# Attention and a SiLU feed-forward on one core: scores computed key-major, exponentials without a shift under a checked bound, SiLU on ScalarE, and an instruction order written by hand

## The chip, the cores and the metric

The kernel runs on 1 of the cores of a Trainium2 chip. The metric is the device time of one execution in microseconds (us); lower is better. PE is the matrix engine (TensorE) and PEld its weight loads, DVE is VectorE, ACT is ScalarE, POOL is GpSimd, SP is the engine whose queue issues the DMAs.

## The reference

Inputs: q, k, v of shape (8, 12, 448, 64) in float32, gains g_q and g_k of 64 elements, and two weight matrices, w_in (768 x 2048) and w_out (2048 x 768), which arrive as float64.

```python
def rmsnorm(x, g):
    return x / np.sqrt(np.mean(x * x, axis=-1, keepdims=True) + 1e-06) * g
q_n, k_n = rmsnorm(q, g_q), rmsnorm(k, g_k)
scores = (1.0 / np.sqrt(64)) * np.matmul(q_n, k_n.transpose(0, 1, 3, 2))
scores = scores - np.max(scores, axis=-1, keepdims=True)
attn = np.exp(scores)
attn = attn / (np.sum(attn, axis=-1, keepdims=True) + 1e-09)
x = np.matmul(attn, v)                     # then heads side by side: (3584, 768)
h = x @ w_in
out = (h / (1.0 + np.exp(-h))) @ w_out     # (3584, 768), float32
```

The gains come from `np.abs(np.random.randn(64)) + 0.5` with a fixed seed; the largest product of a g_q element with its g_k element is 5.26.

## The kernel before

All products are in float32. Work goes by pairs of heads: two heads of 64 features fill the 128 partitions, so there are 8 batches of 6 pairs, 48 pairs in all, numbered n. S is 448 rows, cut into J = 4 groups of R = 112.

For a pair, `load` brings q, k and v. `normalise` squares the rows on GpSimd, sums on VectorE, raises to the power -0.5 on GpSimd and multiplies on GpSimd. `transpose_qk` puts features on partitions with PE transposes; VectorE evicts them. Then, for each of the four query groups c, `scores` makes a 112 x 448 block for either head with queries on partitions (L204), VectorE takes the row maxima (L208), ScalarE computes exp with that maximum as bias and a row sum (L212), and VectorE divides the rows (L216 to L220). `transpose_attn` turns the block over with eight PE transposes (L230), since the sum over keys needs keys on partitions; VectorE (L233) and ScalarE (L235) evict. After the four groups, `weighted_sum` multiplies by v (L245) and leaves the pair's part of x transposed.

The feed-forward part runs one batch behind. `feed_forward` is a generator: 16 blocks f of the hidden layer, each a chain of 6 products with w_in (L282) and then `silu`, which takes one exp on ScalarE (L263) and four operations on VectorE, among them a reciprocal of a 128 x 448 tile (L265); after that, 3 or 4 tiles of 128 tokens by two halves, each a chain of 16 products with w_out (L294), a copy (L303) and a store. An even batch has 3 such tiles, an odd batch 4, as what is left over of two batches is joined. `fill` draws from the generator so many streamed columns after each piece of attention, so that PE has work while the softmax runs. It has nothing to draw in the first batch. After the last pair the last batch's feed-forward runs alone.

During the first batch the weights are brought in and rounded from float64 to float32 in 40 pieces (`load_weights`, `round_weights`: one ScalarE, four VectorE and one GpSimd operation a piece, L123 to L141). The order of instructions on an engine comes from a scheduler, which starts from the order of the code and moves instructions by its own costs.

In float32 a product is two instructions on PE (L282: 768 products, 1536 instructions); a transpose is one.

Of the kernel before, what the change touches and what calls it, by code (L numbers as in the profile page):

```python
# [17 lines left out]
# High words of float64 read as float32: that of 2**-127, and the last one under 2**128's.  # L18
HIGH_MIN = 2.0**-15
HIGH_MAX = 122880.0 - 2.0**-7  # L20


@with_exitstack
def kernel(
# [18 lines left out]
    B, H, S, D = q.shape  # L43
    DM, DFF = w_in.shape
    P = 128
    J = 4  # rows of a sequence that stand side by side on one partition
    R = S // J
    NPAIR = H // 2
    NW = DM // P
    NF = DFF // P  # L50
    HALF = DM // 2
    FULL = S // P  # whole token tiles of a batch; what is over is joined with the next batch's
    REST = S - FULL * P
    assert 2 * D == P and J * R == S and 2 * REST == P and NW == NPAIR and B % 2 == 0

    const = ctx.enter_context(tc.tile_pool(name="const", bufs=1))
    ld = ctx.enter_context(tc.tile_pool(name="ld", bufs=2))
    at = ctx.enter_context(tc.tile_pool(name="at", bufs=2))
    mp = ctx.enter_context(tc.tile_pool(name="mp", bufs=2))
# [5 lines left out]
    ident = const.tile([P, P], F32, name="ident")  # L65
    make_identity(nc, ident)
    minus_half = const.tile([P, 1], F32, name="minus_half")
    nc.gpsimd.memset(minus_half, -0.5)
    # Both gains and the scale of the scores, as one factor per feature of a pair of heads.
# [3 lines left out]
    for t, g in ((gq2, g_q), (gk2, g_k)):  # L73
        for half in range(2):
            nc.sync.dma_start(t[ds(half * D, D), :], g.rearrange("(d one) -> d one", one=1))
# [5 lines left out]
    W1 = const.tile([P, NW, DFF], F32, name="W1")  # L81
    W2 = const.tile([P, NF, DM], F32, name="W2")
    COLS = 512
    pieces = [
        (W1[:, c, ts(i, COLS)], w_in[ts(c, P), ts(i, COLS)])
        for i in range(DFF // COLS)
        for c in range(NW)
    ] + [(W2[:, f, :], w_out[ts(f, P), :]) for f in range(NF)]
    raws = []
    # The second part's own tile, which nothing needs before the weights are there.  # L90
    stage = mp.tile([P, NF * FULL * P], F32, name="g_own", bufs=1).bitcast(I32)
    NRAW, NLOW = 3, 2
    assert NRAW * 2 * DM + NLOW * DM == NF * FULL * P

    def load_weights():
        """The next piece as it comes: float32 to its place, bits of float64 to the stage."""
        if len(raws) == len(pieces):
            return
        dst, src = pieces[len(raws)]
        raw = None  # L100
        if src.dtype == I64:
            raw = stage[:, ds(len(raws) % NRAW * 2 * DM, 2 * dst.shape[-1])]
# [279 lines left out]
```

## Time and profile before

| | before |
|---|---|
| runs (us) | 1970.28, 1974.19, 2138.64; median 1974.19 |
| profiled execution | span 1967.9 us from first to last instruction; the profile has no other time for it |
| busy | PE 1812.2 us, PEld 920.5, DVE 1347.9, ACT 511.9, POOL 437.9 |
| first product of the feed-forward (L282) | at 235.10 us |
| last batch's feed-forward alone, from | 1809.16 us |

The two close runs lie 2.4 and 6.3 us above the span. The span has three stages: the first batch's attention with the rounding of the weights, up to 235 us; the attention of batches 1 to 7 with the feed-forward of batches 0 to 6 between it, 1574 us; and the last feed-forward, 159 us. Rows of the timeline give the start and the length of a group of instructions; since matmuls overlap at their ends, the step from one group's start to the next is what counts.

### The profile page before, as it was taken

The numbers are of one execution on the slowest core, as the hardware profiler recorded it, in microseconds if no ns is written. First come the engines' busy times: TensorE is split into PE (matmuls) and PEld (weight loads), VectorE is DVE, ScalarE is ACT, GpSimd is POOL, SyncE is SP. The second block draws the span as 40 slices with busy tenths as digits, with TensorE's granted clock in tenths as the row PEclk, the third lists the DMA queues.
The fourth block names the chain that finished last, engine by engine and source line by source line (L and its number), as shares of the span: only waits on it lengthen the run. The fifth ranks groups of instructions, "written<-read, shape, count | busy, mean of one in ns | idle before, by whom it ended". The sixth has DMA issues, their size and how long they took to land.

```text
span 1967.9 us, 18858 instructions
## 1 busy us (share of the span) xinstructions
PE 1812.2 (92%) x6784; PEld 920.5 (47%) x6784; DVE 1347.9 (68%) x2433; ACT 511.9 (26%) x1233; POOL 437.9 (22%) x335
## 2 busy tenths in 40 slices
PE   3654899999999999999999999999999999999999
PEld 2222344554445544454445544454445544454555
DVE  6999699538973499637983389745994379843930
ACT  2333222222222232222222222222222223222100
POOL 5567312211221211211121131121112111210000
PEclk9755799999999999999999999999999999999999
DMA  4454000100000000110001010010001000000000
GB/s 147 147 163 163 28 14 15 37 27 18 24 23 31 27 29 14 32 31 18 15 23 36 26 30 17 19 40 23 14 15 40 27 23 19 14 13 13 0 12 20
DMA packets 48796, 70.42 MB, mean 36 GB/s; under 512 B 4160, under 2 KB 43584, under 8 KB 48704
## 3 DMA queue, kind: packets, MB, share of 16 engines
q1 hardware_dynamic: 48704, 69.22, 11.4%
q8 instruction: 54, 0.88, 0.2%
q14 instruction: 38, 0.31, 0.1%
HBM read 58.20 MB, written 11.01 MB: 35 GB/s over the span
## 4 chain that ended last, share of the span: by engine, by line
PE 52%; DVE 38%; ACT 6%; POOL 2%; issue 1%; DMA 1%; SPq 0%; ACTq 0%; POOLq 0%
PE mm L294 24%; DVE s L265 12%; PE mm L282 11%; PE sc L204 6%; PE tr L230 6%; ACT e L212 5%; DVE nmax L208 5%; DVE e L220 5%; PE mm L245 5%; DVE g_own L271 2%; DVE qT L192 2%; DVE s L264 2%; DVE aT L233 2%; DVE total L216 1%; DVE x L261 1%; DVE rms L168 1%
## 5 line engine op out<-in xcount | busy, mean ns | idle before, releaser
L282 PE MATMUL mm<-xT,W 128*128 128x448 f32 x1536 | 627.6, 553 | 0.0
L294 PE MATMUL mm<-W,g_own 128*128 128x384 f32 x1536 | 530.3, 492 | 0.0
L208 DVE TENSOR_REDUCE nmax<-sc 112x1 f32<-112x448 f32 x384 | 224.2, 615 | 306.8 <-PE sc L204 306.4
L282 PEld LDWEIGHTS mm<-xT,W 128*128 128x128 f32 x1536 | 281.1, 192 | 286.3 <-issue 286.3
L212 ACT ACTIVATE e<-sc,nmax 112x448 f32<-112x448 f32 x384 | 241.0, 631 | 537.1 <-DVE nmax L208 533.2
L265 DVE RECIPROCAL s<-s 128x448 f32<-128x448 f32 x128 | 377.1, 2946 | 2.4
L294 PEld LDWEIGHTS mm<-W,g_own 128*128 128x128 f32 x1536 | 279.3, 190 | 209.4 <-issue 47.2
L230 PE MATMUL tr<-ident,e 112*112 112x112 f32 x1536 | 204.2, 276 | 91.6 <-DVE e L220 53.3
L230 PEld LDWEIGHTS tr<-ident,e 112*112 112x112 f32 x1536 | 160.7, 141 | 224.6 <-issue 131.7
L204 PE MATMUL sc<-kT,qT 64*112 64x448 f32 x768 | 226.9, 623 | 40.3 <-ACT e L212 38.2
L167 POOL TENSOR_TENSOR qn<-q 112x512 f32<-112x512 f32 x48 | 51.2, 1066 | 944.4 <-PE tr L188 938.3
L173 POOL TENSOR_TENSOR rms<-rms,minus_half 112x8 f32<-112x8 f32 x96 | 168.2, 1761 | 282.3 <-DVE rms L169 282.2
L235 ACT COPY aT<-tr 112x448 f32<-112x448 f32 x192 | 101.9, 530 | 374.9 <-PE tr L230 374.9
L233 DVE COPY aT<-tr 112x448 f32<-112x448 f32 x192 | 115.9, 604 | 84.6 <-PE tr L230 84.5
L220 DVE TENSOR_SCALAR e<-e,total 112x448 f32<-112x448 f32 x384 | 167.4, 478 | 4.7
L245 PE MATMUL mm<-aT,v 112*64 112x448 f32 x768 | 160.9, 562 | 0.3 <-DVE aT L233 0.3
L263 ACT ACTIVATE s<-x 128x448 f32<-128x448 f32 x128 | 73.5, 574 | 227.9 <-DVE x L261 227.9
L204 PEld LDWEIGHTS sc<-kT,qT 64*112 64x112 f32 x768 | 61.8, 181 | 142.9 <-issue 65.8
L216 DVE TENSOR_SCALAR total<-total 112x2 f32<-112x2 f32 x192 | 49.0, 255 | 100.4 <-ACT e L212 100.4
L245 PEld LDWEIGHTS mm<-aT,v 112*64 112x64 f32 x768 | 53.2, 141 | 103.9 <-issue 71.3
L294 PE MATMUL mm<-W,g_joint 128*128 128x384 f32 x256 | 87.8, 490 | 0.0
L261 DVE TENSOR_SCALAR x<-mm 128x448 f32<-128x448 f32 x128 | 78.2, 611 | 8.7 <-PE mm L282 8.3
(35 smaller groups left out, 983.3 us busy)
## 6 DMA issues: line engine op xcount, KB each, us to landing
g_own<-in_moe_w_in_dram SPq DMA_DIRECT2D x24, 512.0 KB, 4.0
g_own<-in_moe_w_out_dram SPq DMA_DIRECT2D x16, 768.0 KB, 4.5
q<-in_q_dram SPq DMA_DIRECT2D x48, 224.0 KB, 2.6
k<-in_k_dram SPq DMA_DIRECT2D x48, 224.0 KB, 2.7
v<-in_v_dram SPq DMA_DIRECT2D x48, 224.0 KB, 2.6
out_dram<-o SPq DMA_DIRECT2D x56, 192.0 KB, 1.9
gq<-in_g_q_dram SPq DMA_DIRECT2D x2, 0.2 KB, 2.3
gk<-in_g_k_dram SPq DMA_DIRECT2D x2, 0.2 KB, 2.3
```

What stands on the lines that cost most here:

```text
L173: nc.gpsimd.tensor_tensor(out=flat, in0=flat, in1=minus_half[0:R].to_broadcast([R, 2 * J]), op=ALU.pow)
L204: nc.tensor.matmul(ps[h], st["qT"][r, ts(c, R)], st["kT"][r, :], start=True, stop=True)
L208: nc.vector.tensor_reduce(out=nmax[:, h : h + 1], in_=ps[h], axis=AX.X, op=ALU.max, negate=True)
L212: nc.scalar.activation(e, ps[h], AF.Exp, bias=nmax[:, h : h + 1], accum_out=total[:, h : h + 1])
L220: nc.vector.tensor_scalar_mul(out=e, in0=e, scalar1=total[:, h : h + 1])
L230: nc.tensor.transpose(ps[:, j, :], st["e"][h][:, ts(j, R)], ident[0:R, 0:R])
L233: nc.vector.tensor_copy(dst, ps)
L235: nc.scalar.copy(dst, ps)
L245: nc.tensor.matmul(ps[ds(h * D, D), :], st["v"][:, h, j, :], st["aT"][h][:, j, :], start=(j == 0), stop=(j == J - 1),)
L265: nc.vector.reciprocal(out=s, in_=s)
L282: nc.tensor.matmul(h, W1[:, c, ts(f, P)], xT[b][:, c, :], start=(c == 0), stop=(c == NW - 1))
L294: nc.tensor.matmul(ps, g[:, f, :], W2[:, f, ts(half, HALF)], start=(f == 0), stop=(f == NF - 1),)
```

## The change

- **A branch at run time.** The largest product of the gains is computed on chip and compared with 7.5. If it is not above, the scores cannot exceed 60 and `bounded` runs; else `general`, which keeps the row maxima and the old softmax and is not interleaved by hand.
- **Key-major scores.** In `bounded` a score block has keys on partitions: `scores` makes 112 keys x 448 queries for both heads into two PSUM banks, and one ScalarE exp of 112 x 896 evicts it. No maxima, no sum, no division there and no transposes of the attention: `weigh` multiplies the block by v directly.
- **Sums and division.** `add_up` adds the four blocks of a head, head 0 on VectorE and head 1 on GpSimd. `divide` multiplies the sums by a tile of ones on PE, so that the sum stands in all 64 partitions of a head, takes the reciprocal on VectorE (128 x 448, once a pair) and multiplies the unloaded product with it.
- **SiLU on ScalarE** in one function, straight from PSUM, as two activations (384 and 64 columns). The output copies go to VectorE.
- **Rounding** moves one VectorE operation to ScalarE (the absolute value), works in 56 pieces, and is spread over the first ten pairs: 2 pieces a pair in batch 0, 12 a pair after that. Raw w_in lies in the space of w_out until that is needed.
- **PSUM**: scores 2 x 2 banks, `tr` 1, `av` 1, `mm` 2 (before: 2, 2, and 4 for `mm`).
- **Order**: no scheduler moves instructions; each engine runs them as the code issues them. Queries are permuted inside a batch, and the stores undo that, in two DMAs a tile.

The core of the diff, new code only (what it replaces is printed above):

```diff
+    taken = nc.values_load(small[:1, :1], min_val=0, max_val=1)
+    with tc.If(taken > 0) as cond:
+        with tc.manual_schedule():
+            bounded(**arm())
+    with cond.Else():
+        general(**arm())
...
+    def transpose(n, name):
+        t = ps.tile([P, S], F32, name="tr")
...
+        if name == "q":
+            nc.vector.tensor_copy(dst, t)
+        else:
+            nc.vector.tensor_scalar_mul(out=dst, in0=t, scalar1=gains)
+    def scores(n, half):
+        st = state[n]
+        for j in range(2 * half, 2 * half + 2):
+            banks = ps.tile([R, 2, BANK], F32, name="sc", bufs=2)
+            for h in range(2):
+                r = ds(h * D, D)
+                nc.tensor.matmul(banks[:, h, 0:S], st["kT"][r, ts(j, R)], st["qT"][r, :],
+                                 start=True, stop=True)
+            st["e", j] = at.tile([R, 2, S], F32, name="e", bufs=5)
+            nc.scalar.activation(st["e", j], banks[:, :, 0:S], AF.Exp)
+    def weigh(n, half):
+        if half == 0:
+            st["av"] = ps.tile([P, S], F32, name="av")
+        for j in range(2 * half, 2 * half + 2):
+            for h in range(2):
+                nc.tensor.matmul(st["av"][ds(h * D, D), :], st["v"][:, h, j, :],
+                                 st["e", j][:, h, :], start=(j == 0), stop=(j == J - 1))
+    def add_up(n, half):
+        for h, eng in ((0, nc.vector), (1, nc.gpsimd)):
+            es = st["es"][h]
+            if half == 0:
+                eng.tensor_tensor(out=es, in0=st["e", 0][:, h, :], in1=st["e", 1][:, h, :], op=ALU.add)
+            else:
+                for j in (2, 3):
+                    eng.tensor_tensor(out=es, in0=es, in1=st["e", j][:, h, :], op=ALU.add)
+    def unload(n):
+        nc.scalar.copy(st["xU"], st["av"])
+    def divide(n):
+        t = ps.tile([P, S], F32, name="tr")
+        for h in range(2):
+            nc.tensor.matmul(t[ds(h * D, D), :], ones[0:R, :], st["es"][h], start=True, stop=True)
+        r = at.tile([P, S], F32, name="r")
+        nc.vector.reciprocal(out=r, in_=t)
+        nc.vector.tensor_tensor(out=xT[b][hp], in0=st["xU"], in1=r, op=ALU.mult)
...
+            for dst, cols in (
+                (own[:, f, :], ds(odd * z.REST, z.FULL * P)),
+                (joint[:, f, ds(odd * z.REST, z.REST)], ds((1 - odd) * z.FULL * P, z.REST)),
+            ):
+                nc.scalar.activation(dst, h[:, cols], AF.Silu)
...
+    for n, (b, hp) in enumerate(pairs):
+        rounds = [1, 0, 1, 0] if b == 0 else [3, 3, 3, 3]
+        load(n + 2)
+        scores(n, 0)
+        for _ in range(rounds[0]):
+            weights.round(weights.NRAW)
+        fill()
+        if n > 0:
+            divide(n - 1)
+            if hp == 0:
+                begin(b - 1, 4 * z.NPAIR - 1)
+        weigh(n, 0)
+        scores(n, 1)
+        add_up(n, 0)
+        for _ in range(rounds[1]):
+            weights.round(weights.NRAW)
+        fill()
+        transpose(n + 1, "q")
+        weigh(n, 1)
+        unload(n)
+        add_up(n, 1)
+        for _ in range(rounds[2]):
+            weights.round(weights.NRAW)
+        fill()
+        transpose(n + 1, "k")
+        normalise(n + 2)
+        for _ in range(rounds[3]):
+            weights.round(weights.NRAW)
+        fill()
+    divide(last)
```

How the order changes is seen best on three engines.

PE, in a stretch where the feed-forward multiplies by w_out. Before, one query group and a half of a pair (`sc` are the scores, `tr` transposes, `mm` the feed-forward; a row counts products):

```order
L204 MATMUL sc<-kT,qT 112x448 x2
L294 MATMUL mm<-W_92,g_own 128x384 x4
L188 MATMUL tr<-ident,qn 128x112 x4
L188 MATMUL tr<-ident,kn 128x112 x4
L294 MATMUL mm<-W_92,g_own 128x384
L230 MATMUL tr<-ident,e_5081 112x112 x4
L230 MATMUL tr<-ident,e_5084 112x112 x4
L294 MATMUL mm<-W_92,g_own 128x384 x4
L204 MATMUL sc<-kT,qT 112x448 x2
```

After, a whole pair (`av` is the product with v, `tr<-es,ones` the sum product):

```order
L316 MATMUL sc<-qT,kT 112x448 x4
L402 MATMUL mm<-W_82,g_own 128x384 x9
L365 MATMUL tr<-es,ones 64x448 x2
L330 MATMUL av<-e,v_63 64x448 x4
L316 MATMUL sc<-qT,kT 112x448 x4
L402 MATMUL mm<-W_82,g_own 128x384 x9
L302 MATMUL tr<-ident,qn 128x112 x4
L330 MATMUL av<-e,v_63 64x448 x4
L402 MATMUL mm<-W_82,g_own 128x384 x9
L302 MATMUL tr<-ident,kn 128x112 x4
L402 MATMUL mm<-W_82,g_own 128x384 x9
```

The feed-forward comes in four runs a pair instead of eight, the transposes of e are gone, and a run of nine products stands between the scores and the product that needs their exponentials.

ACT, in a stretch where the feed-forward multiplies by w_in. Before (`s` is the exp of the SiLU, `e` that of the scores, `aT` an evicted transpose):

```order
L212 ACTIVATE e_5379,total<-sc,nmax 112x448
L212 ACTIVATE e_5382,total<-sc,nmax 112x448
L263 ACTIVATE s<-x 128x448
L235 COPY aT_5352<-tr 112x4x112
L263 ACTIVATE s<-x 128x448
L212 ACTIVATE e_5448,total<-sc,nmax 112x448
L212 ACTIVATE e_5451,total<-sc,nmax 112x448
```

After (`g_own` and `g_joint` are the SiLU's outputs, `xU` the unloaded product):

```order
L321 ACT_TABLE_LOAD
L321 ACTIVATE e<-sc 112x896 x2
L394 ACT_TABLE_LOAD
L394 ACTIVATE g_own<-mm 128x384
L394 ACTIVATE g_joint<-mm 128x64
L321 ACT_TABLE_LOAD
L321 ACTIVATE e<-sc 112x896 x2
L394 ACT_TABLE_LOAD
L394 ACTIVATE g_own<-mm 128x384
L394 ACTIVATE g_joint<-mm 128x64
L394 ACTIVATE g_own<-mm 128x384
L394 ACTIVATE g_joint<-mm 128x64
L356 COPY xU<-av 128x448
```

Exp and SiLU need different function tables, so a table load stands at each change between them; before, there was one in the whole program. The branch that runs has 88.

DVE, in the first batch. Before (`W` are weights being rounded):

```order
L216 TENSOR_SCALAR total<-total 112x2
L130 TENSOR_SCALAR W_91<-W_91 128x512
L217 RECIPROCAL total<-total 112x2
L130 TENSOR_SCALAR W_91<-W_91 128x512
L220 TENSOR_SCALAR e_244<-e_244,total 112x448
L220 TENSOR_SCALAR e_247<-e_247,total 112x448
L138 SCALAR_TENSOR_TENSOR W_91<-g_own,W_91 128x512 x2
L233 COPY aT_167<-tr 112x4x112
L208 TENSOR_REDUCE nmax<-sc 112x1 x2
```

After, one pair:

```order
L121 TENSOR_SCALAR W_81<-W_81 128x512
L124 TENSOR_SCALAR W_81<-W_81 128x512
L128 SCALAR_TENSOR_TENSOR W_81<-W_82,W_81 128x512
L369 RECIPROCAL r<-tr 128x448
L371 TENSOR_TENSOR xT<-xU,r 128x448
L346 TENSOR_TENSOR es<-e 112x448
L306 COPY qT<-tr 128x448
L351 TENSOR_TENSOR es<-es,e 112x448 x2
```

A piece of rounding now stands ahead of the reciprocal and another ahead of the eviction of the next pair's keys (L308); in the first batch they are 12 pieces instead of 40.

More of the change, by code (lines that the diff above doesn't have):

```diff
@@ new lines @@
+    weights = Weights(nc, const, w_in, w_out, z)
+    for _ in range(weights.NRAW):
+        weights.load()
+    ident = const.tile([P, P], F32, name="ident")
+    make_identity(nc, ident)
+    ones = const.tile([P, D], F32, name="ones")
+    nc.gpsimd.memset(ones, 1.0)
+    minus_half = const.tile([P, 1], F32, name="minus_half")
+    nc.gpsimd.memset(minus_half, -0.5)
+    small = const.tile([1, 1], I32, name="small")
+    most = const.tile([1, 1], F32, name="most")
+    both = const.tile([1, D], F32, name="both")
@@ L76 @@
-    nc.vector.scalar_tensor_tensor(
-        out=gains, in0=gq2, scalar=float(D) ** -0.5, in1=gk2, op0=ALU.mult, op1=ALU.mult
-    )
[L81 to L91, printed above, removed]
```

515 lines of the change are left out of this document (340 added, 175 removed).

## The prediction, made before the changed kernel ran

> **What bounds the kernel now.** I read the page's busy shares first, then the slices over time, then a table of stretches.
>
> ```profile
> PE 1812.2 (92%) x6784; PEld 920.5 (47%) x6784; DVE 1347.9 (68%) x2433; ACT 511.9 (26%) x1233; POOL 437.9 (22%) x335
> PE   3654899999999999999999999999999999999999
> DVE  6999699538973499637983389745994379843930
> PEclk9755799999999999999999999999999999999999
> 17.00:235.00 218.00, 132.21 (x445) 62.04 (x446) 192.32 (x374) 76.97 (x170) 127.36 (x81) 0.68 0.41 130
> 235.00:1812.00 1577.00, 1525.81 (x5893) 773.67 (x5892) 1080.07 (x1971) 419.24 (x1036) 300.59 (x240) 0.99 0.08 24
> ```
>
> There are two limits. In the first five slices, the first batch, PE is half idle at a clock of 0.5 to 0.7 and VectorE is full (192 of 218 us: rounding and softmax). From 235 us on PE is busy for 1526 of 1577 us at clock 0.99: whatever leaves PE there leaves the time. A busy PE is not yet a priced one, so I price its steps from the starts of groups on PE's own timeline, in the middle of the program and around its ends.
>
> ```profile
> 1051.04 1.01 PE L204 MATMUL sc<-kT,qT 64*112 64x448 f32 x4
> 1051.98 3.49 PE L294 MATMUL mm<-W,g_own 128*128 128x384 f32 x10
> 1055.31 0.55 PE L188 MATMUL tr<-ident,qn 112*128 112x112 f32 x4
> 1055.69 0.55 PE L188 MATMUL tr<-ident,kn 112*128 112x112 f32 x4
> 1056.08 0.82 PE L294 MATMUL mm<-W,g_own 128*128 128x384 f32 x2
> 1056.92 1.09 PE L230 MATMUL tr<-ident,e 112*112 112x112 f32 x8
> 1057.85 2.76 PE L294 MATMUL mm<-W,g_own 128*128 128x384 f32 x8
> ...
> 1064.89 3.23 PE L245 MATMUL mm<-aT,v 112*64 112x448 f32 x16
> 1068.05 0.98 PE L230 MATMUL tr<-ident,e 112*112 112x112 f32 x8
> 1068.87 4.05 PE L294 MATMUL mm<-W,g_own 128*128 128x384 f32 x12
> ...
> 235.10 3.19 PE L282 MATMUL mm<-xT,W 128*128 128x448 f32 x8
> 1809.16 61.15 PE L282 MATMUL mm<-xT,W 128*128 128x448 f32 x162
> 1949.80 14.35 PE L294 MATMUL mm<-W,g_own 128*128 128x384 f32 x44
> ```
>
> From these: a w_in instruction takes 61.15/162 = 0.377 us, a w_out instruction 14.35/44 = 0.326. Four score instructions, both heads at once, take 1051.98 - 1051.04 = 0.94 us; the 16 with v 3.16; a set of q or k transposes 0.38 or 0.39; eight transposes of e 0.93 or 0.82, say 0.87. Ten w_out instructions cost 3.33 us from start to start, 0.07 more than 10 x 0.326: a restart of the feed-forward costs about 0.1.
>
> A pair of before then costs 4 x 0.94 + 3.16 + 0.77 + 4 x 0.87 + 8 x 0.1 = 11.97 us of PE. The seven feed-forwards between 235.10 and 1809.16: w_in 7 x 192 x 0.377 = 507; w_out 4 x 192 x 0.326 + 3 x 256 x 0.326 = 501. With 42 pairs, 503, the sum is 1511 of 1574 us. So **63 us there are waits**. The waits of PE in that stretch name most:
>
> ```profile
> PE tr L230 <- DVE qT L192: 28.0, 19, 2.1
> PE tr L230 <- DVE e L220: 21.6, 58, 0.9
> ```
>
> Both are waits of the transposes of e, for the divided block and for the eviction queued with it on VectorE.
>
> **Stage 2, step by step.** The transposes of e go: 4 x 0.87 = 3.48 us a pair. The scores keep their streams (eight blocks a pair, two at a time) but come in two runs of 8 instructions: 0.94 and another 0.75 (two streams of 0.377), so 1.69 a run, 3.38 a pair for 3.76. The product with v is split in two, 3.16 + 0.1. Transposes of q and k are split, 0.77 + 0.1. The sum product is new: two chains side by side, like four score instructions, 0.94. Restarts fall to four, 0.4. The pair: 3.38 + 3.26 + 0.87 + 0.94 + 0.4 = 8.85 us. Saved: 42 x (11.97 - 8.85) = **131 us**.
>
> Now the waits. Feed-forward runs last (507 + 501)/(7 x 23 fills) = 6.3 us. Between the scores and the product that reads their exponentials stands such a run, so I cost the exponentials at nothing if ScalarE gets them out within it. The rows for that:
>
> ```profile
> L212 ACT ACTIVATE e<-sc,nmax 112x448 f32<-112x448 f32 x384 | 241.0, 631 | 537.1 <-DVE nmax L208 533.2
> L123 ACT ACTIVATE g_own<-g_own 128x512 int32<-128x512 uint32 x24 | 16.1, 671 | 66.4 <-POOL W L141 52.2 <-DMA g_own<-in_moe_w_in_dram 14.2
> L123 ACT ACTIVATE g_own<-g_own 128x768 int32<-128x768 uint32 x16 | 14.6, 913 | 28.3 <-POOL W L141 25.7 <-DMA g_own<-in_moe_w_out_dram 2.6
> L303 ACT COPY o<-mm 128x384 f32<-128x384 f32 x56 | 26.8, 479 | 114.3 <-PE mm L294 112.8
> L123 ACT ACT_TABLE_LOAD x1 | 1.3, 1283 | 0.7 <-PEq L366 0.7
> ```
>
> No row has an exp of 896 elements: twice 631 is the upper end, 631 itself the lower; the two L123 rows differ by 0.242 us for 256 elements, so 631 + 448 x 0.945 = 1.05 us, which I take. A SiLU block: 0.48 (the 384-element copy) plus some 0.2 for 64 elements. In a pair that multiplies by w_in, ScalarE then has 4 x 1.05 + 0.53 (unload) + 5.3 blocks x 0.68 + 4 table loads x 1.28 = 13.5 us of about 33. After the scores its longest sequence is a table load and two exponentials, 3.4 us, inside the 6.3; if a SiLU stands ahead too, 4.1. `mm` has two banks instead of four: a chain of six products lasts 4.5 us, and the SiLU of the chain before it ends within 1 us, or 5 us where exponentials stand ahead of it, in which case 3.3 us of attention lie on PE as well. That should hold.
>
> VectorE and `tr`, which has one bank for the q transposes, the k transposes and the sums:
>
> ```profile
> L265 DVE RECIPROCAL s<-s 128x448 f32<-128x448 f32 x128 | 377.1, 2946 | 2.4
> L271 DVE TENSOR_TENSOR g_own<-x,s 128x384 f32<-128x384 f32 x128 | 69.8, 545 | 0.1
> L196 DVE TENSOR_SCALAR kT<-tr,gains 128x448 f32<-128x448 f32 x48 | 30.7, 639 | 0.0
> L138 DVE SCALAR_TENSOR_TENSOR W<-g_own,W 128x512 int32<-128x512 int32 x24 | 17.9, 750 | 0.0
> L130 DVE TENSOR_SCALAR W<-W 128x512 int32<-128x512 int32 x24 | 11.6, 488 | 0.0
> L127 DVE TENSOR_SCALAR W<-W 128x512 f32<-128x512 f32 x24 | 10.4, 441 | 0.0
> L141 POOL TENSOR_TENSOR W<-W,g_own 128x512 int32<-128x512 int32 x24 | 33.0, 1378 | 40.9 <-DVE W L138 27.5 <-DVE total L216 8.8 <-ACT aT L235 3.8
> L173 POOL TENSOR_TENSOR rms<-rms,minus_half 112x8 f32<-112x8 f32 x96 | 168.2, 1761 | 282.3 <-DVE rms L169 282.2
> ```
>
> The reciprocal holds `tr` for 2.95 us; the next user, the q transposes, comes 1.6 + 1.7 + 6.3 us later, so it is hidden; the 128 reciprocals of the SiLU become 48. A pair costs VectorE 2.95 + 0.55 + 6 small operations of about 0.6, below 10 us of 33.
>
> The tight pairs are those from 6 to 9, where the other 44 pieces are rounded. A piece takes 2 x 0.67 us on ScalarE, 0.44 + 0.49 + 0.75 = 1.68 on VectorE, 1.38 on GpSimd; for pair 6, 12 pieces: 16 us, 20 us and 17 us on top of 13, 9 and 9. Each stays under PE's 33, but pieces now stand ahead of reciprocals. I followed pair 6: the reciprocal starts behind three pieces, at 9.5 us, and the first feed-forward chain waits 2.8 us for its last operand. w_out pieces, of 384 elements, are lighter. I take **20 us of waits** in all of stage 2 (4 in pair 6, 16 elsewhere) with bounds of 0 and 110: nothing waits, or the 63 of before remain and pairs 6 to 9 take another 12 each.
>
> Stage 2: 507 + 501 + 42 x 8.85 + 20 = **1400 us** for 1574.
>
> **Stage 1.** Before, six pairs ran in (235 - 17)/6 = 36.3 us each, held by VectorE. Now VectorE has two pieces and one pair, 3.4 + 10 = 13 us, and the chain decides. Its clock: PE was at half speed here, so scores take 3.0 us a run and v 3.1. The chain from the first scores: j0's exp ends at 2.9, j1's at 4.4; the ScalarE part of a piece at 5.7, VectorE's at 7.4; the reciprocal behind it at 10.35, and the q transposes wait for its bank; then v for the second half up to 14.3, unload 14.9, the second piece on ScalarE 16.3 and VectorE 18.0, and only then the eviction of the next keys, 18.7. With handovers between engines I take 19 us a pair, 114 for six. At full clock the same chain gives 17.4 without handovers; a floor is VectorE's 13, and a third more on everything is 25: **84 to 150 us** with the start.
>
> The start itself:
>
> ```profile
> 6.68 1.04 POOL L167 TENSOR_TENSOR qn<-q 112x512 f32<-112x512 f32 x1 [5.38 <-DMA q<-in_q_dram]
> 17.29 1.84 PE L204 MATMUL sc<-kT,qT 64*112 64x448 f32 x4 [1.11 <-DVE kT L196]
> ```
>
> Normalising began at 6.68 us on the arrival of q and scores at 17.29. Now it also waits for the gains, three small VectorE operations, a register load and a branch on every engine. The trace has no such branch; between nothing and another such 10 us I take 3. So pair 0 starts at 20, pair 6 at 134; before, the feed-forward started at 235. Saved: 101 us.
>
> **Stage 3.** 192 x 0.377 + 256 x 0.326 = 156 us, the same instructions; 1809.16 + 156 leaves 2.9 us for the last copy and store. The last reciprocal (2.95 + 0.55) lies beside five of the first chain's products. 159 us, half a microsecond more than nothing lost.
>
> **The sum.** 20 + 114 + 1400 + 159 = 1693 us of span, 275 less than 1967.9: 131 from PE work, 43 from waits, 101 from the first stage. The median of the runs is 6.3 above the span; this gives **1699 us**.
>
> **A rule that speaks against it.** 88 table loads stand where one stood; by the row they are 88 x 1.28 = 113 us, all on an engine that was busy for 26%. The Trainium skill, page "ScalarE: Activation LUTs", section "What ACT_TABLE_LOAD costs", puts every switch at about 2.66 us, as a drain of 1.38 comes on top of 1.28, and advises grouping calls by table set. The load itself agrees with this row (1283 ns); no run here shows the drain. By that price, an estimate from the page, a w_in pair would need 19 us of ScalarE instead of 13.5 and only pairs 6 and 7 would come out over PE's time, by about 15 us in all: 1714.
>
> **The rivals.**
> - *Table switches reach PE.* If every switch delays an exponential or frees a bank late, 88 x 1.28 = 113 us come back: 1812 us. For it: they stand right ahead of the exponentials in ScalarE's order. Against: 13.5 of 33 us.
> - *The first batch stays long*, its in-order chain waiting on rounding as before: 6 x (36.3 - 19) = 104 us more, 1803. For it: two pieces stand in each pair's chain. Against: 12 pieces instead of 40.
> - *Slower: the runs of feed-forward don't cover the exponentials.* It decides once ScalarE is more than 6.3 us late with them; then PE runs the stage 1 chain and the fills one after the other, 18.7 + 24 = 42.7 us a pair for 33: 42 x 9.9 = 416 us more, 2115. Against: waits of this kind (L204 and L230 on ACT or DVE) were 50 us before with less distance.
> - *The branch takes `general`.* It would need a gain product above 7.5, and the largest is 5.26. Without interleaving, 48 pairs of some 20 us, eight feed-forwards of about 146 and 56 pieces of some 1.4 us come to 2200.
>
> **How the numbers follow.** The forecast has 0.85, table switches 0.07, the long first batch 0.05, slower 0.02, `general` 0.01. The range takes in the bounds of the unknown costs: down to no waits and the short first stage, 1699 - 20 - 30 = 1649; up to 90 more of waits, 1789, or 36 more of the first stage with half of those, so I end it at 1790. Left out are the 0.15 of the rivals and a little of the forecast with both bounds at once. Within 2% (about what a measurement of this kernel can tell from no change: 1935 to 2014) only the first two rivals together reach, 1699 + 113 + 104 = 1916 and a slow rounding stage: 0.02. Slower has the last two, 0.03; faster 0.95.
>
> **What would show it.** Right: w_in products begin near 137 us; from there on PE is at 98% or more with a clock of 0.99, L316 and L330 show hardly any wait for ACT, and the last feed-forward begins near 1534 and takes 159. Wrong: waits of PE for L321 (table switches, or fills too short) or for L306 and L308 (rounding ahead of evictions); a first stage of pairs above 25 us; a pair's PE work above 8.85 in the timeline, which would make the 131 us too large.

## The result, and the profile after

| | before | after |
|---|---|---|
| median (us) | 1972.24 (1968.46 to 2138.64, 4 runs) | 1707.88 (1707.17 to 1709.11, 4 runs) |
| ratio after/before | | 0.8671, 95% interval 0.8658 to 0.8683 |
| span of the profiled execution | 1967.9 | 1707.3 |
| time of that execution | 1970.28 | 1709.11 |

The run of 2138.64 us was a slow one, and the ratio leaves it out. The forecast was 1699 us, with a range of 1649 to 1790. It holds, 9 us low. `bounded` was the branch taken: only its lines appear in the trace.

First the page of after: busy shares, and two rows of the slices.

```profile
PE 1609.5 (94%) x5440; PEld 792.0 (46%) x5440; DVE 577.3 (34%) x708; ACT 438.9 (26%) x696; POOL 583.5 (34%) x448
PE   4668688999999999999999999999999999999998
PEclk9878888999999999999999999999999999999999
```

VectorE's 1348 us have become 577, and PE has 203 us less to do. Of the opening, seven slices of 43 us are below nine tenths now, none but the first below six; before, four slices of 49 us were at three to six tenths, most of them at a granted clock of 0.5 to 0.7, which is now 0.7 to 0.9. Cut at pair 0's scores, pair 6's scores, the last wait of PE and the last feed-forward, the table of stretches reads (columns: stretch, its length, busy time and instructions of PE, PEld, VectorE, ScalarE and GpSimd, granted clock of PE, DMA share, GB/s):

```profile
18.93:124.90 105.97, 68.73 (x261) 24.29 (x261) 79.21 (x94) 39.22 (x55) 81.24 (x59) 0.81 0.36 107
124.90:281.30 156.40, 118.33 (x352) 51.73 (x353) 109.49 (x153) 78.99 (x141) 85.60 (x70) 0.85 0.35 99
281.30:1546.65 1265.35, 1265.35 (x4373) 629.67 (x4371) 376.43 (x441) 310.96 (x469) 407.77 (x306) 1.00 0.10 29
1546.65:1707.30 160.65, 155.11 (x450) 84.96 (x448) 8.50 (x11) 9.68 (x32) 0.00 (x0) 0.99 0.04 12
```

From 281 us to the last feed-forward PE is busy without a gap at full clock: nothing there can be won but by less PE work. Whatever was lost against the forecast was lost before 281 us, in pairs 0 to 9. PE's waits by cause (total us, times, longest) and the starts on its timeline that mark the stages:

```profile
PE mm L386 <- ACT g_joint L394: 31.7, 5, 11.0
PE sc L316 <- DVE kT L308: 24.4, 7, 5.6
PE tr L302 <- POOL qn L287: 15.4, 1, 15.4
PE tr L302 <- DVE r L369: 10.4, 5, 2.6
PE mm L386 <- DVE xT L371: 6.4, 1, 6.4
PE tr L302 <- DVE qT L306: 3.2, 4, 1.1
PE av L330 <- ACT e L321: 0.9, 1, 0.9
```

```profile
106.97 3.33 PE L316 MATMUL sc<-qT,kT 64*112 64x448 f32 x8 [3.87 <-DVE kT L308]
124.90 3.30 PE L316 MATMUL sc<-qT,kT 64*112 64x448 f32 x8 [3.35 <-DVE kT L308]
132.33 4.03 PE L386 MATMUL mm<-xT,W 128*128 128x448 f32 x10
```

The 15.4 us are the start. L308, L302 and L306 belong almost wholly to the first batch, whose pairs are 17.9 us apart (124.90 - 106.97) instead of 36.3. The first two rows that matter beyond it are the new ones: **38 us in which the feed-forward waits**, 31.7 of them for a SiLU (L394): `mm` has two banks, and PE can't begin the next chain of products before the SiLU has read one. Between 124 and 290 us no other wait of PE is above 3.3.

Why a SiLU of 0.7 us is 11 us late is told by ScalarE's timeline at the longest of the five waits, with PE's row under it and then rows of GpSimd and of VectorE (in brackets the idle time ahead of a row, and what ended it):

```profile
177.33 0.56 ACT L119 ACTIVATE last<-raw 128x384 int32<-128x384 uint32 x1 [9.94 <-POOL W L132]
177.79 0.54 ACT L120 ACTIVATE W<-raw 128x384 f32<-128x384 f32 x1
178.34 1.28 ACT L394 ACT_TABLE_LOAD   x1
179.63 0.49 ACT L394 ACTIVATE g_own<-mm 128x384 f32<-128x384 f32 x1
180.02 0.22 ACT L394 ACTIVATE g_joint<-mm 128x64 f32<-128x64 f32 x1
```

```profile
180.29 3.35 PE L386 MATMUL mm<-xT,W 128*128 128x448 f32 x4 [11.01 <-ACT g_joint L394]
```

```profile
168.68 1.11 POOL L287 TENSOR_TENSOR qn<-q,rms 112x512 f32<-112x512 f32 x1
169.75 1.03 POOL L287 TENSOR_TENSOR kn<-k,rms 112x512 f32<-112x512 f32 x1
170.75 2.66 POOL L132 TENSOR_TENSOR W<-W,W 128x512 int32<-128x512 int32 x2
...
176.31 0.99 POOL L132 TENSOR_TENSOR W<-W,last 128x384 int32<-128x384 int32 x1 [0.94 <-issue]
```

```profile
167.40 0.43 DVE L124 TENSOR_SCALAR W<-W 128x512 int32<-128x512 int32 x1
...
168.93 3.37 DVE L124 TENSOR_SCALAR W<-W 128x512 int32<-128x512 int32 x1
```

A w_out piece begins on ScalarE by writing `last`, a scratch tile in two slots, and ends on GpSimd, where L132 reads it. The third w_out piece of a group therefore waits on ScalarE until GpSimd has finished the first (176.31 + 0.99 = 177.30; ScalarE goes on at 177.33). ScalarE runs in order, so the SiLU that PE waits for stands behind that piece, though its own input was ready long before: PE had done its last product ahead of the wait by 169.28 (180.29 - 11.01).

### The profile page after: what moved, and what is told of

It reads as the page before. It is cut to its first block, busy times and chain, and to the rows that moved or that the text cites. A ratio compares the mean times of both kernels' runs of the same rounds, so it can differ in the third digit from the quotient of the medians.

```text
span 1707.3 us, 14310 instructions
## 1 busy us (share of the span) xinstructions
PE 1609.5 (94%) x5440; PEld 792.0 (46%) x5440; DVE 577.3 (34%) x708; ACT 438.9 (26%) x696; POOL 583.5 (34%) x448
## 3 DMA queue, kind: packets, MB, share of 16 engines
HBM read 58.20 MB, written 11.01 MB: 41 GB/s over the span
## 4 chain that ended last, share of the span: by engine, by line
PE 87%; DVE 8%; POOL 2%; ACT 2%; issue 1%; DMA 0%; SPq 0%; POOLq 0%; ACTq 0%; DVEq 0%
PE mm L402 35%; PE mm L386 32%; PE sc L316 9%; PE av L330 7%; PE tr L365 2%; PE tr L302 2%; DVE W L124 1%; DVE W L128 1%; DVE es L351 1%; DVE r L369 1%; DVE W L121 1%; POOL rms L280 1%; DVE es L346 0%; POOL sq L274 0%; POOL W L132 0%
## 5 line engine op out<-in xcount | busy, mean ns | idle before, releaser
L386 PE MATMUL mm<-xT,W 128*128 128x448 f32 x1536 | 606.4, 549 | 38.1 <-ACT g_joint L394 31.7
L321 ACT ACTIVATE e<-sc 112x896 f32<-112x896 f32 x192 | 166.5, 914 | 505.9 <-PE sc L316 395.2
L369 DVE RECIPROCAL r<-tr 128x448 f32<-128x448 f32 x48 | 141.9, 2956 | 285.8 <-PE tr L365 285.8
L316 PE MATMUL sc<-qT,kT 64*112 64x448 f32 x768 | 182.1, 595 | 24.4 <-DVE kT L308 24.4
L330 PE MATMUL av<-e,v 112*64 112x448 f32 x768 | 168.6, 561 | 0.9 <-ACT e L321 0.9
L351 POOL TENSOR_TENSOR es<-es,e 112x448 f32<-112x448 f32 x96 | 128.0, 1333 | 88.9 <-ACT e L321 84.7
L280 POOL TENSOR_TENSOR rms<-rms,minus_half 112x16 f32<-112x16 f32 x48 | 139.7, 2910 | 48.4 <-DVE rms L277 48.4
L346 POOL TENSOR_TENSOR es<-e 112x448 f32<-112x448 f32 x48 | 56.6, 1180 | 252.2 <-PE tr L365 249.1
L394 ACT ACTIVATE g_own<-mm 128x384 f32<-128x384 f32 x128 | 62.6, 489 | 280.3 <-PE mm L386 279.5
L316 PEld LDWEIGHTS sc<-qT,kT 64*112 64x112 f32 x768 | 64.6, 183 | 127.3 <-issue 85.8
L308 DVE TENSOR_SCALAR kT<-tr,gains 128x448 f32<-128x448 f32 x48 | 32.7, 682 | 197.9 <-PE tr L302 197.9
L275 DVE TENSOR_REDUCE rms<-sq 112x8 f32<-112x512 f32 x96 | 65.4, 682 | 73.9 <-POOL sq L274 73.9
L330 PEld LDWEIGHTS av<-e,v 112*64 112x64 f32 x768 | 52.2, 141 | 81.1 <-issue 66.5
L306 DVE COPY qT<-tr 128x448 f32<-128x448 f32 x48 | 29.8, 622 | 167.3 <-PE tr L302 167.3
L321 ACT ACT_TABLE_LOAD x44 | 56.5, 1283 | 106.0 <-PE sc L316 58.8
```

The costliest lines, as they stand in the source:

```text
L275: nc.vector.tensor_reduce(out=rms[:, i], in_=sq, axis=AX.X, op=ALU.add)
L280: nc.gpsimd.tensor_tensor(out=flat, in0=flat, in1=minus_half[0:R].to_broadcast([R, 4 * J]), op=ALU.pow)
L316: nc.tensor.matmul(banks[:, h, 0:S], st["kT"][r, ts(j, R)], st["qT"][r, :], start=True, stop=True,)
L321: nc.scalar.activation(st["e", j], banks[:, :, 0:S], AF.Exp)
L330: nc.tensor.matmul(st["av"][ds(h * D, D), :], st["v"][:, h, j, :], st["e", j][:, h, :], start=(j == 0), stop=(j == J - 1),)
L346: eng.tensor_tensor(out=es, in0=st["e", 0][:, h, :], in1=st["e", 1][:, h, :], op=ALU.add)
```

## The experiments

Ratios are to the kernel before, run on the same chip.

### Four slots for the scratch tile

```diff
-last = self.raw_pool.tile([128, n], I32, name="last", tag="last", bufs=2)
+last = self.raw_pool.tile([128, n], I32, name="last", tag="last", bufs=4)
-st["e", j] = at.tile([R, 2, S], F32, name="e", bufs=5)
+st["e", j] = at.tile([R, 2, S], F32, name="e", bufs=4)
```

> Change: the buffer 'last' of the rounding of w_out pieces gets 4 slots instead of 2; e gets 4 instead of 5 to make room. Theory (PE waits 31.7 us in pairs 7 to 9 because the third piece of a group waits on ScalarE for GpSimd to free a slot of 'last', with the SiLUs queued behind it): those waits of L386 on ACT fall to below 8 us and the time falls by 25 to 32 us, to 1676-1683 us. Rival (the rounding as a whole is too slow there: raw slots, DMA or GpSimd set the pace): the same waits stand under another name, on raw DMAs or on VectorE, and the time stays within 8 us of 1708.

Measured: 1687.22 us (1686.18 to 1689.22), ratio 0.8562 (0.8547 to 0.8578), 20.7 less than the changed kernel and the fastest version of the study. ScalarE's waits for the slot of `last` in the changed kernel, between 125 and 290 us:

```profile
ACT last L119 <- POOL W L132: 40.3, 10, 9.9
```

Here, PE's waits for the SiLU and ScalarE's two waits at the same line:

```profile
PE mm L386 <- ACT g_joint L394: 11.8, 4, 7.2
ACT last L119 <- DMA raw<-in_moe_w_out_dram: 25.3, 12, 6.0
ACT last L119 <- POOL W L132: 0.6, 1, 0.6
```

PE's 31.7 us became 11.8, and the time fell by about as much. The cause is shown, with one correction: ScalarE hardly waits for the slot of `last` any more but, at the same line, for the raw piece to arrive (25.3 us instead of 7.3). Three of the four waits of PE that are left, 10.6 of the 11.8 us, end at a SiLU that stands behind such arrivals.

A fourth slot for raw pieces, paid for with `e` in three buffers:

```diff
-op = weights.raw_pool = ctx.enter_context(tc.tile_pool(name="op", bufs=3))
+op = weights.raw_pool = ctx.enter_context(tc.tile_pool(name="op", bufs=4))
-st["e", j] = at.tile([R, 2, S], F32, name="e", bufs=4)
+st["e", j] = at.tile([R, 2, S], F32, name="e", bufs=3)
```

> The changed kernel with `last` in four slots, the pool of raw pieces and outputs in four slots instead of three, and `e` in three buffers (to make room). With `last` in four slots alone PE still waited 11.8 us for the SiLU of pairs 7 to 9, and ScalarE stood 25 us there for arriving raw pieces (11 or 12 waits, longest 6.0). Theory: loads can't be issued before a raw slot comes free, so a fourth slot takes most of that: PE's wait for L394 below 5 us, time 1677 to 1682. Rival: the pieces are then held by VectorE and GpSimd, which need 1.7 and 1.4 us for each, or the exponentials by their three buffers: the wait moves to another line and the time stays at 1684 to 1690.

Measured: 1703.16 us, ratio 0.864 (0.8625 to 0.8654), 16 worse than without it. Waits of PE for exponentials:

```profile
PE av L330 <- ACT e L321: 15.1, 8, 3.9
```

and ScalarE at one of the exponentials:

```profile
152.92 0.92 ACT L321 ACTIVATE e<-sc 112x896 f32<-112x896 f32 x1 [9.77 <-DVE es L346]
```

Neither forecast holds as a whole. Three buffers are too few for `e`: an exponential now waits 9.8 us until the sums have read the oldest block, and PE's waits for exponentials go from 0.9 to 15.1 us, 12 of them in the first batch. Pair 6 starts at 134.56 us instead of 125.27, so 9 of the 16 us are lost before it. Between 125 and 290 us ScalarE's waits for raw pieces fall from 25.3 to 8.5, but PE's for the SiLU stay at 11.7. Whether a fourth raw slot alone would help is open; no run had the room for it.

### The feed-forward ahead of the rounding

At each of the four places of a pair:

```diff
+        fill()
         for _ in range(rounds[0]):
             weights.round(weights.NRAW)
-        fill()
```

> Change: in each quarter of a pair the feed-forward run (with its SiLUs) is issued ahead of the pieces of rounding instead of behind them; nothing else. Theory (SiLUs queued behind a blocked rounding piece on ScalarE hold the two mm banks): the SiLUs now pass ahead, the blocked piece delays only the next exponentials, which have 6 us of cover; waits of L386 on ACT fall by 20 to 30 us, and L330 waits on ACT for a few us instead: 1680-1692 us. Rival (rounding sets the pace of pairs 6 to 9): the wait moves to L330 or L316 on ACT or VectorE in full, 1700-1715 us.

Measured: 1701.93 us, ratio 0.8634 (0.8619 to 0.8648). PE's waits between 125 and 290 us:

```profile
PE av L330 <- ACT e L321: 8.5, 2, 4.8
PE tr L302 <- DVE r L369: 7.6, 3, 5.0
PE sc L316 <- DVE kT L308: 5.1, 3, 3.3
PE mm L402 <- POOL W L132: 4.3, 1, 4.3
```

The SiLU's wait is gone, and most of it came back as waits for whatever now stands behind the pieces: the exponential, the reciprocal, the keys (3.3 of their 5.1 us were there before), the last rounded piece of w_out. The wait for pair 6's last operand is as before, 6.5. This order alone buys 6 us, the slots 20.7.

### The keys ahead of the second piece

```diff
         transpose(n + 1, "q")
         weigh(n, 1)
         unload(n)
+        transpose(n + 1, "k")
         add_up(n, 1)
         for _ in range(rounds[2]):
             weights.round(weights.NRAW)
         fill()
-        transpose(n + 1, "k")
         normalise(n + 2)
```

> Change: the transposes of the next pair's keys and their eviction are issued ahead of the second group of sums and the second piece of rounding, in every pair. Theory (in the first batch the eviction of the next keys stands behind a piece of rounding and two sums on VectorE, and the next scores wait for it: 24.4 us in 7 waits): those waits go, six pairs of 17.9 us become 14 to 15, and the time falls by 15 to 24 us, to 1684-1693 us; nothing changes from pair 10 on. Rival (the chain goes on through unload, rounding and the reciprocal's bank, so something else is late right behind it): less than 8 us, 1700-1708 us.

Measured: 1709.39 us, ratio 0.8673 (0.8658 to 0.8687): no change. The waits say why:

```profile
PE sc L316 <- DVE kT L308: 5.4, 7, 0.8
PE tr L302 <- DVE r L369: 31.5, 5, 6.9
```

19 us went from L308 and 21 came to L302: the transposes need the one bank of `tr`, which the reciprocal of the pair before (2.96 us, behind its own piece) has not read yet. The first batch is a ring through that bank: with one link moved, the next one shows.

A further run put the pieces behind the division too, with four slots for `last`:

```diff
-        for _ in range(rounds[0]):
-            weights.round(weights.NRAW)
-        fill()
         if n > 0:
             divide(n - 1)
             if hp == 0:
-                begin(b - 1, 4 * z.NPAIR - 1)
+                begin(b - 1, 4 * z.NPAIR)
+        for _ in range(rounds[0]):
+            weights.round(weights.NRAW)
+        fill()
```

(beside the slots of `last` and `e` and the move of the keys, both as above).

> Change: four slots of 'last' (e with four), the next keys' transposes ahead of the second piece of rounding, and the sum product with its reciprocal ahead of the first piece. Theory (moving the keys alone did nothing because the wait went to the reciprocal, which stands behind the first piece and holds the bank of the q transposes: L302 on L369 went from 10.4 to 31.5 us; with both moved the chain loses both): pairs of the first batch fall from 17.9 to 13-15 us, the first wait for xT (5.5 us) goes, and the time is 1660-1672 us, 15 to 27 below the run with four slots alone. Rival (the first batch is held by something else right behind, such as GpSimd's normalising at 9 us a pair or the rounding): pairs stay above 16.5 us and the time is 1678-1690.

Measured: 1706.16 us, ratio 0.8656 (0.8644 to 0.8668), 19 worse than the four slots alone. Its largest wait:

```profile
PE tr L302 <- POOL qn L287: 48.2, 6, 15.3
```

With the division earlier too, the normalised queries became the late link: apart from the 15.3 of the start, 5.8 to 6.9 us in each of the last five pairs of the first batch, which are 19.2 us apart instead of 17.9. The span is 16.6 us longer than with the four slots alone. Of that 2 come from the first batch (pair 6 starts at 127.32 instead of 125.27) and 5 from more idle time of PE up to 290 us. In the rest of that time PE got through 422 instructions instead of 462, at a granted clock of 0.88 to 0.93 instead of 0.90 to 0.94; how much of this is the clock and how much the mix of instructions was not separated. The edit of `begin` also deals a batch's feed-forward out in 24 runs instead of 23, and what that does was not run by itself.

### GpSimd's share of the sums

```diff
-        for h, eng in ((0, nc.vector), (1, nc.gpsimd)):
+        for h, eng in ((0, nc.vector), (1, nc.vector)):
```

> Change: both heads' sums of exponentials on VectorE, none on GpSimd. Theory (PE is the only limit from pair 10 on; VectorE is busy for 30% there): no change from pair 10 on, PE has no idle time there; in the first batch VectorE has three more additions of 0.6 us a pair in the chain but GpSimd is free for the rounding, which also shortens the waits for 'last' in pairs 7 to 9: 1690-1715 us in all, and single additions on VectorE drop from 0.76-1.44 us to about 0.62 since GpSimd no longer reads beside them. Rival (VectorE close to its limit): 20 us or more longer, with PE waits for L306, L308 or L369 in all pairs.

Measured: 1705.41 us, ratio 0.8655 (0.864 to 0.867): as the changed kernel. VectorE's groups between 300 and 1546 us, of the changed kernel and then of this one:

```profile
L346 DVE TENSOR_TENSOR es<-e 112x448 f32<-112x448 f32 x38 | 58.2, 1532 | 0.0
L351 DVE TENSOR_TENSOR es<-es,e 112x448 f32<-112x448 f32 x76 | 47.9, 630 | 4.1
```

```profile
L346 DVE TENSOR_TENSOR es<-e 112x448 f32<-112x448 f32 x76 | 43.8, 618 | 0.0
L351 DVE TENSOR_TENSOR es<-es,e 112x448 f32<-112x448 f32 x152 | 91.3, 621 | 5.6 <-DVE es L351 0.5
```

The first addition takes 1.53 us where GpSimd adds beside it, and 0.62 without that. The second and third, which come after GpSimd has finished, take 0.63 in the changed kernel too. Twice as many additions on VectorE cost 29 us more there (135.1 for 106.1), and the time doesn't notice.

### No table switches

```diff
-                nc.scalar.activation(dst, h[:, cols], AF.Silu)
+                nc.scalar.activation(dst, h[:, cols], AF.Exp)
```

> Change: the feed-forward's activation is exp instead of SiLU, so that no table is switched between it and the softmax; the result is another function, the instructions have the same shapes. Theory (88 table loads lie beside PE's work): ScalarE's busy time falls by 87 x 1.28 = 112 us and the time by 0 to 8 us (a little in pairs 6 to 9, where ScalarE is nearly full): 1700-1708 us. Rival (switches delay the exponentials): 20 us or more less. By the Trainium skill's price of 2.66 us a switch (page 'ScalarE: Activation LUTs') the loads with their drains would be 234 us of ScalarE.

Measured: 1705.79 us in one run, 2 less. One load is left of 88, and ScalarE is busy for 325.8 us instead of 438.9:

```profile
L321 ACT ACT_TABLE_LOAD x1 | 1.3, 1283 | 20.9 <-PE sc L316 20.9
PE mm L386 <- ACT g_joint L394: 30.7, 5, 10.0
```

113 us of ScalarE are gone and the SiLU's wait is still 30.7: the switches lie beside PE's work, and they don't cause that wait either.

### The order left to the scheduler

```diff
-        with tc.manual_schedule():
-            bounded(**arm())
+        bounded(**arm())
```

> Change: the same code of the bounded branch, but the scheduler may move instructions, as it does before the change; the order by hand is undone alone. Theory (the gain is PE work and a short first batch, both from the computation, and the order by hand gives the rest): PE's busy time within 20 us of 1609; some 20 to 60 us of waits of PE more: 1725-1770 us. Rival 1 (the order by hand is the gain): above 1800 us. Rival 2 (the scheduler does as well): 1690-1715 us.

Measured: 1705.48 us in one run, the same as with the hand order. Waits of PE (lines are one lower here):

```profile
PE av L329 <- ACT e L320: 42.7, 14, 7.7
PE mm L385 <- ACT g_joint L393: 5.3, 3, 2.5
```

The scheduler puts the pieces elsewhere, so that the wait for the SiLU is nearly gone, and pays with exponentials that stand behind pieces, most of it in the first batch. After that PE is the limit in both. My expectation of 20 to 60 us was wrong: by this run the change gets nothing from the hand order as it is.

### The branch

```diff
-SCORE_MAX = 60.0
+SCORE_MAX = 6.0
```

> Change: the bound on the scores is lowered to 6, so that the check on chip fails and the other branch runs. The prediction put this branch at 2200 us: 48 pairs of some 20 us not covered by the feed-forward, eight feed-forwards of 146 us, 56 pieces of rounding ahead of everything. Rival: the scheduler overlaps a batch's feed-forward with the next batch's softmax although the code does not interleave them, PE stays near 90% busy from the end of the rounding on, and the time is 1900-2020 us.

Measured: 2693.65 us in one run, 493 above the price of that rival. PE's first scores, rows of the stretches (first feed-forward, then the next batch's attention) and the starts of the first and the last feed-forward:

```profile
86.94 1.84 PE L529 MATMUL sc<-kT,qT 64*112 64x448 f32 x4 [59.72 <-DVE kT L521]
```

```profile
297.00:442.00 145.00, 139.91 (x407) 75.93 (x408) 10.24 (x21) 14.71 (x41) 7.42 (x6) 0.98 0.04 12
442.00:607.50 165.50, 129.85 (x411) 65.10 (x410) 78.14 (x190) 45.58 (x121) 36.55 (x30) 0.61 0.08 23
```

```profile
296.88 72.43 PE L590 MATMUL mm<-xT,W 128*128 128x448 f32 x192
2532.70 72.43 PE L590 MATMUL mm<-xT,W 128*128 128x448 f32 x192
```

The feed-forward takes the 146 us of the price, and the first scores start at 87 us, behind the rounding that I had priced at 78. The pairs are what was mispriced: 35 us each in the first batch ((296.88 - 86.94)/6), and 29 in later ones: (2532.70 - 296.88)/7 = 319 a batch, less 145, over 6. I had priced 20. With no feed-forward between its pieces the attention pays twice: PE waits, and its granted clock is 0.61. In the second stretch PE is busy for 21.6 us a pair (129.85/6), where the same products took 11.97 in the kernel before by the prediction's steps.

Without the branch at all (the bound is still computed, but not read, and the key-major path always runs):

> The changed kernel without the branch: the bound isn't read or tested, the key-major path always runs. Theory by the starts of the two traces (scores at 18.93 us for 17.29): the branch and the test cost 1.6 us at the start and nothing later, so 1705 to 1707. Rival: what was predicted, 3 us, or more if code behind the branch loads later: 1700 to 1704.

Measured: 1704.28 us, ratio 0.8649 (0.8635 to 0.8663). Scores start at 18.18 us instead of 18.93, so reading the bound and branching cost 0.8 us there, below both my values. The other 3 us are not at the start, and the intervals of the two kernels overlap.

### Parts of the change in the kernel before

Row maxima and shift left out, transposes of e kept:

```diff
-            nc.vector.tensor_reduce(
-                out=nmax[:, h : h + 1], in_=ps[h], axis=AX.X, op=ALU.max, negate=True
-            )
-                e, ps[h], AF.Exp, bias=nmax[:, h : h + 1], accum_out=total[:, h : h + 1]
+                e, ps[h], AF.Exp, accum_out=total[:, h : h + 1]
```

> One part of the change alone in the kernel before: row maxima and the shift by them are left out (exp of the score itself), all else as it was, transposes of e too. Theory: PE's own work stays, so only waits can go: of the first stage VectorE loses 48 reductions of 0.6 us and pairs shorten by 5 us or so (30 us in six pairs), and later at most 20 of the 63 us of waits, as those stand at the division and the evictions, not at the maxima: 1925 to 1950. Rival: the chain scores, maximum, exp is what held both, and the kernel falls by 80 us or more, below 1890.

Measured: 1903.54 us, ratio 0.9662 (0.9645 to 0.9678), between the two expectations. Stage 2 (the seven interleaved feed-forwards) before, and then here:

```profile
235.10:1809.16 1574.06, 1522.87 (x5884) 772.03 (x5883) 1079.97 (x1971) 418.70 (x1035) 300.59 (x240) 0.99 0.08 24
```

```profile
214.55:1742.86 1528.31, 1506.79 (x5886) 769.21 (x5885) 902.49 (x1638) 387.12 (x1037) 304.34 (x243) 1.00 0.08 25
```

The first stage is 20.5 us shorter and stage 2 45.8: PE's idle time there fell from 51 to 21.5, and the same instructions took 16 less. So more than half of PE's idle time hung on the maxima. Between 240 and 1720 us, PE's waits at L230 for the evicted queries fell from 28.0 to 6.7 us and those for the divided block from 19.9 to 13.2. Before, the maxima stood in VectorE's queue ahead of those evictions and divisions; whether that or the earlier exponential shortened the waits was not separated, and the scheduler was free to set another order.

SiLU as one ScalarE function, maxima kept:

```diff
-        x = mp.tile([P, S], F32, name="x")
-        nc.vector.tensor_scalar_max(out=x, in0=h, scalar1=-87.0)
-        s = mp.tile([P, S], F32, name="s")
-        nc.scalar.activation(s, x, AF.Exp, scale=-1.0)
-        nc.vector.tensor_scalar_add(out=s, in0=s, scalar1=1.0)
-        nc.vector.reciprocal(out=s, in_=s)
-            nc.vector.tensor_tensor(out=dst, in0=x[:, c], in1=s[:, c], op=ALU.mult)
+            nc.scalar.activation(dst, h[:, c], AF.Silu)
```

> Another part alone in the kernel before: SiLU as one ScalarE function instead of clamp, exp, add, reciprocal and product (about 520 us of VectorE's 1348 less, all after the first stage, and ScalarE's table switches added). Theory: after the first stage PE is at 97% and VectorE at 68%, so only a part of the 63 us of waits goes: 1925 to 1965. Rival: without the hand order the switches of ScalarE's tables stand ahead of the exponentials that PE waits for (38 us at L204 before), and the time rises to 1980 or more.

Measured: 1986.8 us, ratio 1.0082 (1.0065 to 1.0099): slower by 17. VectorE has 520 us less to do, and PE waits more, at the same line as before. Between 240 and 1720 us:

```profile
PE tr L230 <- DVE qT L192: 49.1, 27, 2.3
PE tr L230 <- DVE e L220: 14.8, 39, 0.5
```

The first was 28.0 us in 19 waits, the second 19.9 in 53. The scheduler, which sets the order there by its own costs, now draws the feed-forward in other portions. Where it multiplies by w_in, two of its instructions stand between the transposes of k and the next transposes of e, whose banks those of q and k still hold; before, it was four to nine in most pairs. That this order is the whole of the 17 us was not shown. The rival's sign was right, but not its place: the waits at L204 are still 38.2.

## Why the prediction was right, step by step

| term (us) | predicted | measured |
|---|---|---|
| start, to pair 0's scores | 20 | 18.9 |
| first batch, six pairs | 114 | 106.0 |
| stage 2, pair 6's scores to the last feed-forward | 1400 | 1421.8 |
| last feed-forward | 159 | 160.6 |
| time above the span | 6.3 | 0.6 (median; 1.8 in the profiled execution) |
| sum | 1699 | 1707.9 |

- **PE's own work** was the heart of the sum, and it holds. In stage 2, 1421.8 less the 38 us of waits (31.7 + 6.4) is 1384, against the prediction's 507 + 501 + 42 x 8.85 = 1380. With four slots the same account gives 1380: stage 2 lasts 1525.19 - 125.27 = 1399.9, and 19.6 of it are waits.
- **The waits of stage 2** are the term that was mis-sized: 38 us instead of 20, within the bounds of 0 and 110. I gave 4 to pair 6 and 16 to all the rest. Pair 6's wait for its last operand came at 6.4 (I had followed it to 2.8). The others came in pairs 7 to 9, where I had stopped following because "w_out pieces, of 384 elements, are lighter". They are lighter, but they alone use the scratch tile with two slots. I had summed each engine's time for them and not asked how many may be under way at once. The two banks of `mm`, of which I wrote "That should hold", did not: I had asked only for exponentials ahead of the SiLU, not for a blocked piece. The four slots take 20 us of the waits away: that error is shown. A third bank for `mm` was not tried.
- **The first batch**: VectorE's and ScalarE's chain gives 17.9 us a pair instead of 19, close to the 17.4 without handovers. PE's granted clock was 0.81 there rather than the half speed I had counted with (the first scores of a pair do take 3.33 us, as at 106.97, but the second 1.76), and the exp takes 0.914 us (166.5 us for 192) rather than 1.05. Its last link was the keys behind the second piece, as the waits at L308 show; when they were moved, the reciprocal's bank took their place at the same time.
- **The total** is closer than its terms. Stage 2 came out 22 us longer than forecast and the last feed-forward 2; the start, the first batch and the time above the span came out shorter by 1, 8 and 6. That these 15 us cancel most of the 23 is luck.
- **Exponentials hidden by feed-forward runs**: right. The only wait at L330, 0.9 us, lies in pair 0 (at 23 us), where there is no feed-forward yet.
- **Table switches**: right to cost them at nothing; without them it is 2 us less. The rule I weighed against it, on the Trainium skill's page "ScalarE: Activation LUTs", section "What ACT_TABLE_LOAD costs", doesn't show here: in the ScalarE rows above, the operation before ends at 178.33, the load runs from 178.34 for 1.28 us, and the SiLU starts at 179.63. There is no 1.38 us of drain beside it. The prediction's 15 us for that price don't follow from its own rows either: 16 + 19 = 35 us for pair 6 is 2 above PE's 33.
- **The share of the parts.** I split 275 us into 131 of PE work, 43 of waits and 101 of first stage. The traces give 110 for the first stage (235.10 - 124.90) and 152 for stage 2, less 2 at the end. By the steps priced, 131 of the 152 are PE work; by the busy time of the profiles (1522.87 before, 1383.68 after) it is 139, and PE's idle time there fell by only 13, from 51 to 38. The 63 us of waits that the prediction found in the kernel before were thus 12 too many, and PE's work as much too small. Of the single parts, the maxima are worth 66 us in the old kernel and the SiLU nothing by itself. The key-major layout and the spread of the rounding were not run apart from each other.
- **The rivals**: table switches, the long first batch and uncovered exponentials are refuted by the rows above. The price of `general` was too low by 493 us, 471 of them in its pairs (35 and 29 us instead of 20), with both a low clock and waits in them; their shares were not separated.

## What to carry to other kernels

An engine that runs in order turns one missing buffer into lateness of everything queued behind it. Where background work (here the rounding) is mixed into an engine's queue, count the slots that its pieces need as well as the engine's time, and follow the heaviest pairs to the end. Moving a link of such a ring moved most of the wait; more slots removed two thirds of it, and one buffer too few in another ring (three for `e`) lost 16 of those 21 us again. Where PE is without a gap at full clock, time saved on another engine is worth next to nothing: 113 us less on ScalarE gave 2.

## What the runs showed of the hardware

- VectorE is slowed while GpSimd works. The addition of two 112 x 448 tiles takes VectorE 1.53 us beside GpSimd's additions (from 706.30 us of the changed kernel, with GpSimd's from 706.18) and 0.62 alone. At 168.93 us of the changed kernel, an operation on VectorE that takes 0.43 us elsewhere took 3.37, while GpSimd had two products and two additions in a row. The Trainium skill, page "GPSIMD Engine Reference", section "8. Key points", says that the two share their SBUF interfaces and contend where VectorE reads two inputs there or is in a two-port mode; the traces agree for the addition, which reads two, and give the size. The operation at 168.93 reads one tile, and no trace here shows its mode; nor was it separated whether GpSimd is slowed as well.
- GpSimd's power for 16 columns takes 2.91 us (L280, mean of 48), where 8 columns took 1.76: one longer call is cheaper than two.
- In the attention of the branch without interleaving, where PE is busy for 130 of 165.5 us in short pieces, its granted clock was 0.61; in the stretches without gaps it was 0.98 to 1.00.
